# Scaled words of the weight decoder move from a PSUM bank of their own into the ring of the block maxima, the weight product gets both of its ring's banks, and the first stage is issued in another order

## The chip, the cores and the metric

The kernel runs on one core of a Trainium2 chip. The metric is device time in microseconds; 963.3 us is the median of three runs of the kernel before (961.33 to 964.49). The engines are named as the profile names them: PE is TensorE (PEld its weight loads), DVE is VectorE, ACT is ScalarE, POOL is GpSimd, and SP is the queue that issues the DMA transfers.

## The reference

Block-causal attention over 8 batches and 8 heads (576 rows, head width 64, blocks of 64), then a gated MLP without a nonlinearity, on the concatenated heads:

```python
scores = scale * np.matmul(q, k.transpose(0, 1, 3, 2))
scores = np.where(block_i >= block_j, scores, -1000000000.0)
scores = scores - np.max(scores, axis=-1, keepdims=True)
attn = np.exp(scores)
attn = attn / (np.sum(attn, axis=-1, keepdims=True) + 1e-09)
x = np.matmul(attn, v)          # (B, H, S, D), then (B*S, H*D)
a = x @ w1
b = x @ w2
h = a * b @ w3
out = h @ w_out
```

Since nothing nonlinear stands between `w3` and `w_out`, the kernel forms their product once.

## The kernel before

**Two stages.** Heads are handled in pairs, four pairs to a batch. In the first stage the program treats pairs 0 to 3 (batch 0) and prepares all weights; after it, pairs 4 to 31 run interleaved with the MLP of the batches before them, in which TensorE multiplies without a pause. The MLP's tiles are `ab` (line 503) and `o` (line 519).

**What the first stage does with weights.** The weights arrive as raw 64-bit words, in 40 units of 512 KB: 8 of `wout`, 16 of `w3t` (two for each of eight row blocks m), 8 of `w1`, 8 of `w2`. `load_w` (line 209) treats one unit in four steps: the transfer into a `wraw` buffer (a ring of five), ACT's scaled copy `y` of the high words (line 221), two byte fields that ACT and POOL write into `wbits` (lines 222 and 223; two buffers in turn), and DVE's shift-and-or that joins `y` and `wbits` into the float (line 224; a SCALAR_TENSOR_TENSOR in the profile). For `w1` and `w2` the result is split into a high half (POOL) and a low half (DVE), `w1h`, `w1l`, `w2h`, `w2l`. A `wraw` buffer can be refilled only when ACT and POOL have read it.

**What it does with the product.** `gen_prod` (line 474) forms, for each m, eight products over k of `w3` with `wo` in one PSUM bank, `acc`. ACT copies the bank to `wh`, DVE takes the rest `wl = acc - wh`. The next m that uses the same bank has to wait for `wl`.

**What it does with a pair.** The raw q, k, v arrive in one transfer. `shift_mask` (line 241) finds the block maxima: TensorE writes block scores to a PSUM bank of the ring `psq`, DVE reduces them into `m` (10 reductions a pair), TensorE transposes `m`, ACT negates it to `ms`. `prep_qk` (line 289) casts q and k and takes their low halves (`TENSOR_TENSOR qk<-raw,qk`), and shifts copies of them to the other 64 partitions by DMA (`qk<-qk`); for `ms` the same is done (`qk<-ms`). Then come the score tiles (`pss`, called S below), ACT's exponentials (`pe`), the products with v (`psx`), a transpose of the sums on DVE (`tr<-psx`), and the normalized `x32` with its halves `xh` and `xl`.

**PSUM.** Eight banks: two for `pss`, two for `psx`, two for `psq` (maxima), one, `psy`, for `y`, and one, `psm`, for `acc`. After the first stage `psm` and `psy` are used in turn by the MLP's tiles.

**What sets the order.** In the first stage every call of the engines is recorded, not issued. `ORDER`, a list of 768 call numbers written out by hand or by a search, then issues them (line 614); it sets the order on every engine and of the DMA transfers on SP, and, through `Later`, which buffer of a ring a call gets. Each engine takes its instructions in this order, and SP too: a transfer that must wait for an engine holds up all behind it. After the first stage the order comes from `PLAN` and, off TensorE, from the Tile scheduler.

```python
    def load_w(dst, src):
        t = new(tl["early"], [P, 1024], I32, tag="wraw", name="wraw", bufs=5)
        y = new(ps_m, [P, 512], F32, tag="psy", name="y")
```

Of the kernel before, what the change touches and what calls it, by code (L numbers as in the profile page):

```python
# [9 lines left out]
F32 = mybir.dt.float32  # L10
# [8 lines left out]
PSUM = bass.MemoryType.PSUM  # L19
OTHERS = {mybir.EngineType.Activation, mybir.EngineType.DVE, mybir.EngineType.Pool, mybir.EngineType.SP}  # L20

P = 128
# [39 lines left out]
)  # L62

ORDER = [int(k) for k in """
# [20 lines left out]
""".split()]  # L85

RING = {"raw": 2, "pss": 2, "psm": 1, "psy": 1, "psq": 2, "wraw": 5, "wy": 4, "w3": 2, "xh": 8, "xl": 8}

DELAY = 3

# [37 lines left out]
def block_causal_attention__then__gated_mlp_kernel(ctx, tc, qkv, consts, ident_in, w1, w2, w3t, wout, out_t):  # L128
# [5 lines left out]
    def new(pool, shape, dtype, tag, **k):  # L134
        if not isinstance(nc, Held):
            return pool.tile(shape, dtype, tag=tag, **k)
        return Later(lambda: slot(pool, shape, dtype, tag, **k))

    def slot(pool, shape, dtype, tag, name, **k):
        ring = rings[tag]  # L140
        n = RING.get(tag, 1)
        t = ring[-n] if len(ring) >= n else pool.tile(shape, dtype, tag=tag, name=tag, **k)
# [9 lines left out]
    ctx.enter_context(tc.manual_schedule(engines={mybir.EngineType.PE}))  # L152
    ps_s = ctx.enter_context(tc.tile_pool(name="ps_s", bufs=2, space=PSUM))
    ps_x = ctx.enter_context(tc.tile_pool(name="ps_x", bufs=1, space=PSUM))
    ps_m = ctx.enter_context(tc.tile_pool(name="ps_m", bufs=1, space=PSUM))
    ps_q = ctx.enter_context(tc.tile_pool(name="ps_q", bufs=2, space=PSUM))

    both = cpool.tile([P, 2 * P], F32, name="ident")
# [49 lines left out]

    def load_w(dst, src):
        t = new(tl["early"], [P, 1024], I32, tag="wraw", name="wraw", bufs=5)  # L210
        y = new(ps_m, [P, 512], F32, tag="psy", name="y")
        bits = tl["bits"][tl["unit"] % 2]
        tl["unit"] += 1
        nc.sync.dma_start(out=t, in_=src)
        high = t.rearrange("p (c two) -> p c two", two=2)[:, :, 1]
        byte = t.bitcast(U8).rearrange("p (c e) -> p c e", e=8)
        if dst is None:
            dst = new(tl["early"], [P, 512], F32, tag="wy", name="wy", bufs=4)
        low = bits.bitcast(U8).rearrange("p (c e) -> p c e", e=4)[:, :, 0]
        top = bits.bitcast(F8).rearrange("p (c e) -> p c e", e=4)[:, :, 3]  # L220
        nc.scalar.mul(out=y, in_=high.bitcast(F32), mul=2.0**-112)
        nc.scalar.activation(out=top, in_=byte[:, :, 7], func=AF.Copy, bias=127.5 * 2.0**-60, scale=-(2.0**-60), saturate=False)
        nc.gpsimd.tensor_scalar(out=low, in0=byte[:, :, 3], scalar1=1.0 / 32, scalar2=-31.0 / 64, op0=ALU.mult, op1=ALU.add)
        nc.vector.scalar_tensor_tensor(out=dst.bitcast(I32), in0=y.bitcast(I32), scalar=3, in1=bits, op0=ALU.logical_shift_left, op1=ALU.bitwise_or)
        return dst
# [258 lines left out]
            done[0] += 1  # L484
            yield

    turns = itertools.cycle(("psm", "psy"))

    def turn():
        return next(turns)  # L490

    def gen_moe(b):
        mp, gh, gl = tl["late"], tl["gh"], tl["gl"]
        for h in range(2):
            for f in range(NF):
                acc = []
                for a, b2 in ((w1h, w1l), (w2h, w2l)):
                    t = ps_m.tile([P, 512], F32, tag=turn(), name="ab")
                    fs = slice(f * P, (f + 1) * P)
                    for c in range(NC):  # L500
                        xh, xl = x_of[b, c, h]
                        for s, (l, r) in enumerate(((a, xh), (b2, xh), (a, xl))):
                            nc.tensor.matmul(t[:, 0:HALF], l[:, c, fs], r, start=(c == 0 and s == 0), stop=(c == NC - 1 and s == 2))  # L503
                        if c == 1 or (c == NC - 1 and len(acc) == 0):
                            yield
                    acc.append(t)
                a32 = mp.tile([P, HALF], F32, tag="a32", name="a32", bufs=2)
                nc.scalar.copy(a32, acc[0][:, 0:HALF])
                g32 = mp.tile([P, HALF], F32, tag="g32", name="g32", bufs=2)
                nc.vector.tensor_tensor(out=g32, in0=acc[1][:, 0:HALF], in1=a32, op=ALU.mult)  # L510
                nc.scalar.copy(gh[:, f, :], g32)  # L511
                nc.gpsimd.tensor_tensor(out=gl[:, f, :], in0=g32, in1=gh[:, f, :], op=ALU.subtract)  # L512
                yield
            for e in range(DM // P):
                t = ps_m.tile([P, 512], F32, tag=turn(), name="o")
                es = slice(e * P, (e + 1) * P)
                for f in range(NF):
                    for s, (l, r) in enumerate(((wh, gh), (wl, gh), (wh, gl))):
                        nc.tensor.matmul(t[:, 0:HALF], l[:, f, es], r[:, f, :], start=(f == 0 and s == 0), stop=(f == NF - 1 and s == 2))  # L519
                    if f % 2 and f < NF - 1:  # L520
                        yield
                o32 = mp.tile([P, HALF], F32, tag="o32", name="o32", bufs=2)
                nc.scalar.copy(o32, t[:, 0:HALF])
                nc.sync.dma_start(out=out_t[es, b * S + h * HALF : b * S + (h + 1) * HALF], in_=o32)
                yield
# [163 lines left out]
```

## Time and profile before

| | us |
|---|---|
| median of three runs | 963.3 |
| profiled execution, its own time | 965.79 |
| its span | 964.0 |
| first transfer is issued | 0.74 |
| transfers of the first stage | 29.44 MB until 132 us |
| PE busy in the span | 937.7 (97%) |
| DVE busy in the span | 692.4 (72%) |
| ACT busy | 550.2 (57%) |
| POOL busy | 612.4 (64%) |

The profiled execution took 1.8 us more outside its span, and 2.5 us more than the median. In the page's 40 slices of 24 us, TensorE's busy share is in tenths; a 9 in all slices but the first ones says that only the first five or so have idle time on that engine. In the waits view a row reads: engine and instruction that waited, what ended the wait, the total in microseconds, how often, the longest. In the chain view a row is a start, a duration and who held the chain. Line 124 is a helper's, so groups of the first stage are told apart by their tiles.

### The profile page before, as it was taken

To read this page: it belongs to the slowest core of one execution; us is meant where nothing else is said; L and a number is where in the kernel's file an instruction comes from. 1 tells how busy PE (TensorE), PEld (TensorE's weight loads), DVE (VectorE), ACT (ScalarE), POOL (GpSimd) and SP (SyncE) were. 2 spreads that over 40 slices of the span, in tenths; PEclk is the share of its full clock that TensorE was granted. 3 is DMA by queue.
4 is the path that set the end of the run, shared out by engine and by line. 5 is a ranking of instruction groups with operands and counts; after the bars stand their busy time and mean duration, and the time that the engine had idled before them with its cause. 6 is when DMAs were issued, how large, how long until landed. Compare 5 with 4: busy or idle time off the path is not lost.

```text
span 964.0 us, 18369 instructions
## 1 busy us (share of the span) xinstructions
PE 937.7 (97%) x6624; PEld 878.0 (91%) x6624; DVE 692.4 (72%) x1238; ACT 550.2 (57%) x1433; POOL 612.4 (64%) x614
## 2 busy tenths in 40 slices
PE   4889989999999999999999999999999999999998
PEld 2445569999999999999999999999999999999998
DVE  7768887778877777777887777777887877774100
ACT  5767655665666565565565655566556556553221
POOL 4667667676776767676777667676767767672211
PEclk9999999999999999999999999999999999999999
DMA  8668622222122222212122122312212222100000
GB/s 308 220 196 291 195 63 61 79 64 65 49 76 71 64 82 64 82 59 87 32 71 76 59 82 64 89 52 89 60 49 70 70 71 64 50 13 26 7 20 25
DMA packets 31261, 79.86 MB, mean 83 GB/s; under 512 B 5353, under 2 KB 13673, under 8 KB 31171
## 3 DMA queue, kind: packets, MB, share of 16 engines
q1 hardware_dynamic: 31171, 78.70, 26.4%
q8 instruction: 52, 0.85, 0.4%
q14 instruction: 38, 0.31, 0.1%
HBM read 50.76 MB, written 9.44 MB: 62 GB/s over the span
## 4 chain that ended last, share of the span: by engine, by line
PE 90%; DMA 5%; DVE 2%; ACT 2%; issue 1%; SPq 0%; POOL 0%; ACTq 0%; DVEq 0%; POOLq 0%
PE ab L503 42%; PE o L519 21%; PE s L334 9%; PE x L389 9%; PE mx L261 4%; PE psm L124 2%; DMA wraw<-in_w3t 2%; DMA wraw<-in_w 1%; PE psx L124 1%; DMA qk<-qk 1%; PE pss L124 1%; ACT psy L124 1%; ACT wbits L124 0%; PE tot L406 0%; SPq L124 0%
## 5 line engine op out<-in xcount | busy, mean ns | idle before, releaser
L355 POOL TENSOR_TENSOR rsum<-rsum,p 128x448 f32<-128x448 f32 x224 | 186.4, 832 | 87.5 <-ACT p L349 78.5
L352 DVE TENSOR_TENSOR pl<-p,ph 128x448 fp32r<-128x448 f32 x168 | 149.6, 904 | 60.8 <-ACT ph L350 59.9
L512 POOL TENSOR_TENSOR gl<-g,gh 128x288 fp32r<-128x288 f32 x128 | 114.4, 893 | 121.5 <-ACT gh L511 121.5
L503 PE MATMUL ab<-xh,w2h 128*128 128x288 f32 x512 | 153.7, 300 | 0.1
L519 PE MATMUL o<-gh,wh 128*128 128x288 f32 x512 | 153.5, 300 | 0.0
L503 PE MATMUL ab<-xh,w1h 128*128 128x288 f32 x512 | 151.2, 295 | 0.3 <-DVE wl L124 0.3
L503 PE MATMUL ab<-xl,w2h 128*128 128x288 f32 x512 | 151.1, 295 | 0.0
L503 PE MATMUL ab<-xh,w1l 128*128 128x288 f32 x512 | 150.9, 295 | 0.0
L503 PE MATMUL ab<-xl,w1h 128*128 128x288 f32 x512 | 150.9, 295 | 0.0
L503 PE MATMUL ab<-xh,w2l 128*128 128x288 f32 x512 | 150.9, 295 | 0.0
L519 PE MATMUL o<-gh,wl 128*128 128x288 f32 x512 | 150.9, 295 | 0.0
L519 PE MATMUL o<-gl,wh 128*128 128x288 f32 x512 | 150.8, 295 | 0.0
L304 POOL TENSOR_TENSOR qk<-raw,qk 64x1152 fp32r<-64x1152 f32 x54 | 144.2, 2671 | 2.0
L511 ACT CAST gh<-g 128x288 fp32r<-128x288 f32 x128 | 55.4, 433 | 143.2 <-DVE g L510 143.1
L350 ACT ACTIVATE ph<-s 128x288 fp32r<-128x288 f32 x336 | 131.3, 392 | 0.0
L334 PE MATMUL s<-qk 128*128 128x288 f32 (+4 forms) x672 | 129.6, 301 | 0.3 <-DMA qk<-ms 0.3
L349 ACT ACTIVATE p<-s 128x448 f32<-128x448 f32 x224 | 85.4, 381 | 51.1 <-PE s L334 50.3
L352 DVE TENSOR_TENSOR pl<-rsum,ph 128x288 fp32r<-128x288 f32 x112 | 76.3, 683 | 49.2 <-ACT ph L350 46.2
L389 PE MATMUL x<-ph,vs 128*128 128x128 f32 x336 | 110.3, 329 | 0.0
L265 DVE TENSOR_REDUCE m<-mx 128x1 f32<-128x512 f32 (+1 forms) x270 | 107.7, 448 | 1.7
L510 DVE TENSOR_TENSOR g<-ab,a 128x288 f32<-128x288 f32 x128 | 56.6, 442 | 69.3 <-PE ab L503 67.8
L334 PEld LDWEIGHTS s<-qk 128*128 128x128 f32 (+1 forms) x672 | 99.9, 179 | 1.9 <-DMA qk<-ms 0.9
(97 smaller groups left out, 2241.3 us busy)
## 6 DMA issues: line engine op xcount, KB each, us to landing
raw<-in_qkv SPq DMA_DIRECT2D x31, 896.0 KB
qk<-qk SPq DMA_DIRECT2D x124, 144.0 KB
out_t<-o SPq DMA_DIRECT2D x64, 144.0 KB
wraw<-in_w3t SPq DMA_DIRECT2D x16, 512.0 KB
wraw<-in_w SPq DMA_DIRECT2D x16, 512.0 KB
wraw<-in_wout SPq DMA_DIRECT2D x8, 512.0 KB
qk<-ms SPq DMA_DIRECT2D x62, 2.2 KB
raw<-in_qkv SPq DMA_DIRECT2D x2, 288.0 KB
```

What stands on the lines that cost most here:

```text
L265: nc.vector.reduce_max(m[:, col : col + 1], sc, axis=AX.X)
L304: (nc.gpsimd if "late" in tl or n * j else nc.vector).tensor_tensor(out=qk[j][o, 2:4], in0=rqk[o], in1=qk[j][o, 0:2], op=ALU.subtract)
L334: nc.tensor.matmul(t[ks, at : at + q1 - q0], qk[j][:, k, kr], qk[j][:, q, q0:q1], start=(s == 0), stop=(s == 1))
L349: nc.scalar.activation(p32, t[ks, at : at + w], AF.Exp, scale=SCALE)
L350: nc.scalar.activation(ph[ks, o : o + w], t[ks, at : at + w], AF.Exp, scale=SCALE)
L352: nc.vector.tensor_tensor(out=low, in0=p32, in1=ph[ks, o : o + w], op=ALU.subtract)
L355: nc.gpsimd.tensor_tensor(out=r, in0=r, in1=p32, op=ALU.add)
L389: nc.tensor.matmul(xps[:, to : to + w], v[:, c, :], pr[:, a : a + w], start=(u < 2 and s == 0), stop=(u in (0, len(PV) - 1) and s == len(p ...
L503: nc.tensor.matmul(t[:, 0:HALF], l[:, c, fs], r, start=(c == 0 and s == 0), stop=(c == NC - 1 and s == 2))
L510: nc.vector.tensor_tensor(out=g32, in0=acc[1][:, 0:HALF], in1=a32, op=ALU.mult)
L512: nc.gpsimd.tensor_tensor(out=gl[:, f, :], in0=g32, in1=gh[:, f, :], op=ALU.subtract)
L519: nc.tensor.matmul(t[:, 0:HALF], l[:, f, es], r[:, f, :], start=(f == 0 and s == 0), stop=(f == NF - 1 and s == 2))
```

## The change

Three things are changed. `y` is allocated from the ring `psq`, which the block maxima use, so the three uses (scores of the blocks, the transposed maxima, `y`) take turns in two banks; the tag `psy` is gone. The ring `psm` has two banks instead of one: the product uses them in turn in the first stage, and the MLP's tiles use the same two banks in turn afterwards, as before, without the helper that switched tags. And `ORDER` has the same 768 calls in another order.

```diff
-RING = {"raw": 2, "pss": 2, "psm": 1, "psy": 1, "psq": 2, "wraw": 5, "wy": 4, "w3": 2, "xh": 8, "xl": 8}
+RING = {"raw": 2, "pss": 2, "psm": 2, "psq": 2, "wraw": 5, "wy": 4, "w3": 2, "xh": 8, "xl": 8}
...
-    ps_m = ctx.enter_context(tc.tile_pool(name="ps_m", bufs=1, space=PSUM))
+    ps_m = ctx.enter_context(tc.tile_pool(name="ps_m", bufs=2, space=PSUM))
...
-        y = new(ps_m, [P, 512], F32, tag="psy", name="y")
+        y = new(ps_q, [P, 512], F32, tag="psq", name="y")
...
-    turns = itertools.cycle(("psm", "psy"))
-
-    def turn():
-        return next(turns)
-
...
-                    t = ps_m.tile([P, 512], F32, tag=turn(), name="ab")
+                    t = ps_m.tile([P, 512], F32, tag="psm", name="ab")
...
-                t = ps_m.tile([P, 512], F32, tag=turn(), name="o")
+                t = ps_m.tile([P, 512], F32, tag="psm", name="o")
...
 ORDER = [int(k) for k in """
-8 46 0 44 42 1 4 2 7 5 6 52 39 70 47 67 11 57 38 71 13 3 41 12 62 45 97 16 14 43 9 40 69 10 78 75 53 55 17 54 81 18 19 50 49 92 20 198 56 21 48 15 119
+8 46 0 4 1 42 3 6 7 5 2 44 52 39 70 47 11 57 38 71 13 62 41 67 40 92 12 22 23 9 75 43 84 24 30 10 31 45 25 33 18 19 54 55 32 21 14 20 49 50 15 26 27
```

What this does to the engines' order is shown at three places. **The DMA queue at the first half of the stage**, SP, before: transfers into `wraw` are weight units, `qk0<-qk0` is the shift of a pair's q and k that waits for DVE's cast of them, `raw` is the next pair.

```order
L124 DMA wraw_118<-in_w1 128x1024
L124 DMA wraw_124<-in_w3t 128x1024
L124 DMA raw_120<-in_qkv 128x1792
L124 DMA wraw_132<-in_w1 128x1024
L124 DMA wraw_135<-in_w3t 128x1024
L124 DMA wraw_114<-in_w3t 128x1024
L124 DMA qk0_86<-qk0_86 64x576
L124 DMA wraw_118<-in_w1 128x1024
L124 DMA qk0_86<-qk0_86 64x576
```

The same place now, from the transfer of pair 3 on to the shift of pair 2:

```order
L124 DMA raw_131<-in_qkv 128x1792
L124 DMA wraw_119<-in_w1 128x1024
L124 DMA wraw_123<-in_w1 128x1024
L124 DMA wraw_128<-in_w1 128x1024
L124 DMA wraw_134<-in_w1 128x1024
L124 DMA wraw_115<-in_w3t 128x1024
L124 DMA qk0_86<-qk0_86 64x576 x2
L124 DMA wraw_119<-in_w3t 128x1024
```

Before, 16 weight units were issued ahead of pair 2's shift, and the 17th stood behind it; now 21 are issued ahead of it.

**The end of the stage on TensorE**: `psm` is the product's bank, `w3` its left side, `psq<-ident` the transposed maxima of pair 4, `s4_0` the first scores of pair 4, `ab` the MLP's first tile. Before:

```order
L124 MATMUL psq_139<-kb_122,qd_90 128x448
L124 MATMUL psm_241<-wo_94,w3_385 128x512 x6
L124 MATMUL psq_137<-ident_81,m_153 9x128
L124 MATMUL psm_241<-wo_94,w3_385 128x512 x2
L334 MATMUL s4_0_932<-qk0_86 128x288 x2
L334 MATMUL s4_0_938<-qk0_86 128x288 x2
L503 MATMUL ab_944<-xh_380,w1h_82 128x288
```

Now:

```order
L124 MATMUL psm_352<-wo_94,w3_341 128x512
L124 MATMUL psm_221<-wo_94,w3_175 128x512
L124 MATMUL psm_352<-wo_94,w3_341 128x512
L124 MATMUL psq_137<-ident_81,m_146 9x128
L124 MATMUL psm_352<-wo_94,w3_341 128x512 x6
L334 MATMUL s4_0_932<-qk0_86 128x288 x2
L334 MATMUL s4_0_938<-qk0_86 128x288 x2
L498 MATMUL ab_944<-xh_361,w1h_82 128x288
```

Before, all eight products of m = 7 go to the one bank, behind `wl` of m = 6, and `ab` takes that bank again. Now m = 6 (`psm_221`) and m = 7 (`psm_352`) overlap, and `ab` takes the bank of m = 6.

**The same end on DVE**: `wl<-psm` empties a bank, `w3<-ps..` joins the last unit of `w3`, `x32` and `xl` finish pair 3, `qk0<-raw` is the low half of pair 4's q and k. Before:

```order
L124 SCALAR_TENSOR_TENSOR w3_385<-psy_150,wbits0_95 128x512
L124 CAST qk1_87<-raw_103 64x1152
L124 TENSOR_TENSOR wl_85<-psm_241,wh_84 128x512
L124 TENSOR_REDUCE m_153<-psq_137 128x1
L124 STREAM_TRANSPOSE tr_256<-psx_221 64x576
L124 SCALAR_TENSOR_TENSOR w3_385<-psy_150,wbits1_96 128x512
L124 TENSOR_REDUCE m_153<-psq_137 128x1
L124 TENSOR_TENSOR w2l_89<-wy_492,w2h_88 128x512
```

Now, from the last unit of `w3` on:

```order
L124 SCALAR_TENSOR_TENSOR w3_341<-psq_148,wbits1_96 128x512
L124 TENSOR_TENSOR w2l_89<-wy_481,w2h_88 128x512
L124 RECIPROCAL rr_266<-rr_266 128x18
L124 STREAM_TRANSPOSE tr_258<-rr_266 128x576
L124 TENSOR_TENSOR x32_272<-x32_272,tr_258 128x576
L124 TENSOR_TENSOR qk0_86<-raw_103,qk0_86 64x1152
L124 TENSOR_TENSOR wl_85<-psm_221,wh_84 128x512
L124 TENSOR_TENSOR xl_907<-x32_272,xh_900 128x288
L124 TENSOR_TENSOR wl_85<-psm_352,wh_84 128x512
```

The two halves of `w3` for m = 7 stood around the cast of pair 4 and `wl` of m = 6; now that `wl`, with pair 4's q and k, stands behind the last half.

38 rows, old and new, of the table ORDER are left out of this document.

## The prediction

> **What bounds the kernel now.** I read the slices first, then the busy times by stretch, cut where the first scores start (18.68) and where the MLP's first tile starts (132.25).
>
> ```profile
> span 964.0 us, 18369 instructions
> PE   4889989999999999999999999999999999999998
> 0.00:18.68 18.68, 5.12 (x16) 1.84 (x16) 12.66 (x21) 11.05 (x18) 9.84 (x17) 1.00 0.92 325
> 18.68:42.10 23.42, 22.16 (x88) 13.87 (x89) 19.39 (x36) 15.96 (x33) 12.37 (x12) 1.00 0.63 206
> 42.10:73.00 30.90, 25.88 (x83) 12.76 (x81) 21.29 (x36) 21.79 (x42) 19.80 (x25) 0.94 0.63 212
> 73.00:105.37 32.37, 32.37 (x118) 18.44 (x119) 28.83 (x49) 24.96 (x50) 24.41 (x28) 1.00 0.79 276
> 105.37:120.80 15.43, 14.81 (x52) 7.83 (x50) 11.10 (x18) 8.89 (x17) 8.06 (x10) 1.00 0.58 179
> 120.80:132.25 11.45, 9.29 (x26) 4.28 (x26) 9.24 (x17) 6.00 (x14) 5.98 (x7) 1.00 0.11 26
> 132.25:964.00 831.75, 828.05 (x6245) 819.02 (x6245) 589.91 (x1067) 461.60 (x1263) 531.92 (x518) 1.00 0.21 61
> ```
>
> The columns are the stretch, its length, busy time of PE, PEld, DVE, ACT, POOL, granted clock, DMA share, GB/s. Behind 132.25 TensorE is busy 828.05 of 831.75 us, so that part moves as a block: **the change is worth what it moves the start of `ab`**. In the first stage no engine is full. DVE is the fullest over it: 12.66 + 19.39 + 21.29 + 28.83 + 11.10 + 9.24 = 102.5 of 132.25 us. TensorE, from 18.68 on, is busy 104.5 of 113.6 us, a busy time that holds stretched matmuls. So this stage is bound by waits between engines that each take a fixed order. The chain says which end last:
>
> ```profile
> 8.83 8.96 DMA qk<-qk
> 18.68 0.85 PE pss L124 x2
> 105.37 8.06 DMA wraw<-in_w
> 122.86 0.70 DVE wl L124
> 123.61 5.42 PE psm L124 x12
> 132.25 1.86 PE ab L503 x12
> ```
>
> The start is held by a small transfer (8.96 us) that lands behind those issued before it. Later a weight unit that took 8.06 us to land holds it, and at the end TensorE begins m = 7 of the product at 123.61, the moment `wl` has emptied the only bank.
>
> **The start: 0.** Eleven transfers up to that `qk<-qk` are the same set in the new order, with the constants a little earlier; its landing is set by their bytes, and DVE needs only about 12 of its 17.8 us until then. I take no change up to 18.68.
>
> **The end of the stage: -2.3 us.** DVE's last rows, with their waits in brackets:
>
> ```profile
> 124.59 0.69 DVE L124 SCALAR_TENSOR_TENSOR w<-psy,wbits 128x512 int32<-128x512 int32 x1
> 125.66 0.68 DVE L124 TENSOR_TENSOR w2l<-wy,w2h 128x512 fp32r<-128x512 f32 x1
> 126.58 0.27 DVE L124 RECIPROCAL rr<-rr 128x18 f32<-128x18 f32 x1
> 127.37 0.77 DVE L124 STREAM_TRANSPOSE tr<-rr 128x576 f32<-128x576 f32 x1
> 128.24 0.76 DVE L124 TENSOR_TENSOR x<-x,tr 128x576 f32<-128x576 f32 x1
> 129.59 0.65 DVE L124 TENSOR_TENSOR xl<-x,xh 128x288 fp32r<-128x288 f32 x1 [0.59 <-POOL xh L124]
> 131.51 0.69 DVE L124 TENSOR_TENSOR wl<-psm,wh 128x512 fp32r<-128x512 f32 x1 [1.27 <-ACT wh L124]
> L124 DVE TENSOR_TENSOR qk<-raw,qk 64x1152 fp32r<-64x1152 f32 x6 | 8.7, 1457 | 0.1
> ```
>
> From the join of the last `w3` unit (124.59) to `ab` (132.25) it takes 7.66 us now, most of it one bank's chain: `wl` of m = 6, eight products, `wh`, `wl` of m = 7. With two banks, m = 7's first four products run before that join and four behind it: 4 x 2 x 0.45 (5.42 / 12 for one of the two passes of a product) = 3.6 us, ending 0.69 + 3.6 = 4.3 us behind the join's start. Meanwhile DVE does the join, `w2l`, reciprocal, transpose, `x`, and pair 4's low half, which now stands here: 0.69 + 0.68 + 0.27 + 0.77 + 0.76 + 1.46 = 4.6 us. Pair 4's four first scores then take some 0.7 us, and `wl` of m = 6 0.69 us beside them; `ab` no longer waits for `wl` of m = 7. So 5.4 us in place of 7.66. The other half, `xl` and the last `wl`, stands behind: if `ab` found it in its way, it would cost 0.65 + 0.69 = 1.3 us.
>
> **The join itself: from 124.59 to 120.1, -4.5 us.** DVE must do its work ahead of the join, and the rest is idle time. Now: 102.5 less 5.7 behind 124.59 is 96.8 of work, so 27.8 idle. Then: 102.5 less 6.4 is 96.1. The waits that make the idle time, until 132:
>
> ```profile
> DVE wl L124 <- ACT wh L124: 4.1, 3, 2.4
> DVE qk L124 <- PE pss L124: 3.1, 4, 1.1
> DVE wy L124 <- ACT wbits L124: 2.9, 1, 2.9
> DVE w L124 <- ACT psy L124: 2.3, 2, 1.7
> DVE wy L124 <- POOL wbits L124: 2.1, 3, 0.9
> DVE m L124 <- PE psq L124: 1.8, 2, 1.5
> DVE w L124 <- POOL wbits L124: 1.1, 2, 0.7
> PE psm L124 <- DVE wl L124: 3.6, 4, 2.2
> SPq L124 <- DVE qk L124: 26.7, 7, 13.9
> ```
>
> - Start, until 18.68: 18.68 - 12.66 = 6.0. Stays.
> - Weight units (`wy`, `w` behind `wbits`, `psy`): 2.9 + 2.3 + 2.1 + 1.1 = 8.4. They are late because their transfers are issued late: SP stood 26.7 us behind DVE's casts. In the new order four units of `w1` and one of `w3t` go ahead of pair 2's shift. Following the rows by hand from 18.68, each at the end of what it waits for, with the durations above and 7 us for a unit to land, I get these moments:
>
> ```profile
> 52.12 0.56 SPq L124 DMA_DIRECT2D wraw<-in_w  x1
> 57.34 0.81 SPq L124 DMA_DIRECT2D wraw<-in_w  x2
> 107.27 1.56 SPq L124 DMA_DIRECT2D wraw<-in_w3t  x2
> ```
>
>   the 17th unit at 41 in place of 52.12, the 20th at 49 in place of 57.34, the 40th at 103 in place of 107.27. I take 2.7 of the 8.4 as left (-5.7). If nothing came earlier, this term is 0.
> - `wl` behind `wh`: 4.1, less the 1.27 that lies behind the join, 2.8. In the new order `wl` of m = 2 to 5 stand several rows behind their `wh`; 0 left (-2.8).
> - DVE behind TensorE: 3.1 + 1.8 = 4.9. This grows. Two rows of the new order stand across: the transpose of pair 0's second head stands ahead of the first `w3` unit of m = 1, while TensorE first does three products that wait for `wo` (by hand 3.5 us of DVE idle, near 35 to 38), and a reduction for pair 3 waits behind scores whose shift has just been issued (3.4 us, near 73 to 77). With five shorter ones I get 9.6 (+4.7).
> - All else: 27.8 - 6.0 - 8.4 - 2.8 - 4.9 = 5.7, taken as it is.
>
> That is 6.0 + 2.7 + 0 + 9.6 + 5.7 = 24.0 of idle and 96.1 of work: 120.1. (By hand alone the join came at 117.5; the hand count has no gap between an engine's end and the next one's start, and I leave 2.6 us for that and for landings beyond 7 us.)
>
> **The shared ring.** `y` and the maxima now take turns in two banks. The trace of before shows no such sharing. Between two units it helps: ACT's copy into the one bank `psy` waited for DVE's join of the unit before. Between a unit and a maximum it hurts: the block scores, on TensorE, wait for a join on DVE that waits for a landing, and all matmuls queue behind.
>
> ```profile
> ACT psy L124 <- DMA wraw<-in_w: 4.0, 2, 3.4
> ACT wbits L124 <- DMA wraw<-in_w3t: 4.1, 2, 2.2
> ACT wbits L124 <- DMA wraw<-in_w: 3.1, 3, 1.9
> ACT psy L124 <- DMA wraw<-in_w3t: 1.0, 1, 1.0
> ```
>
> ACT waited 12.2 us for landings. The price of sharing lies between 0 (every unit has landed when its turn comes) and +12.2 (each of these waits reaches TensorE). I take it inside the 9.6 above, since with units issued 4 to 11 us earlier most have landed; 12.2 is kept for the range. The product's second bank is worth between 0 and the 3.6 us that `psm` waited for `wl`; 2.2 at most of it is already in the tail.
>
> A transfer's time is thus the number that matters most: 8.06 us above for one unit. The Trainium skill (DMA: Bandwidth & Descriptors, Anatomy of one DMA — SWDGE (gpsimd) path) fits 2.0 us plus bytes over 436 GB/s on the GpSimd path, an estimate of 3.2 us for 512 KB. By that hardly a unit would be late, and the 5.7 us would not be there to win: the outcome that the second rival below prices from rows. Here SP issues, and the row says 8.06, with the DMA share at 0.58 to 0.79; the row decides.
>
> TensorE's clock is 0.94 in 42.10:73.00, 1.00 elsewhere: 0.06 x 30.9 = 1.9 us at most, behind its waits there. The Trainium skill (TensorE: Matmul & The Clock Gate, Part 1: The HAM clock gate) says that an idle window of about 3.4 us halves the clock. By that rule the new order, whose longest TensorE wait by hand is 1.9 us, would win these 1.9 us back, as the first rival below has it, and one gap more would lose as much again; the sum counts neither.
>
> **Sum.** -2.3 - 4.5 = -6.8: `ab` at 125.5. The profiled execution took 965.79, so 959.0 on its own scale; it lies 2.5 above the median of 963.3, so the median goes to **956.5 us**.
>
> **The rivals.**
> - *Larger gain:* TensorE becomes the bound and only its busy time is left. It idled 113.6 - 104.5 = 9.1 us; with these and the clock's 1.9 gone, -11.0: 952.3. For it: DVE's work alone would allow 102.5 plus 6.0. Against: the two places where DVE stands behind TensorE in the new order.
> - *Landings eat it (the order does not do what it says):* units are issued earlier but land no earlier, since the transfers queue (share 0.79 in one stretch already), and only the tail is won: 963.3 - 2.3 = 961.0. For it: the DMA must move the same 29 MB in less time.
> - *Slower:* the shared ring. Landings beyond 10 us at one unit after another keep its bank, the maxima of the next pair wait on TensorE, and with them the product and the scores. All 12.2 us reach TensorE; the tail's 2.3 and the 5.7 stay won: 963.3 + 12.2 - 8.0 = 967.5. It decides from landings 3 us longer than the 7 counted. Against: only one landing in the chain is over 8 us, the start's apart.
>
> **How the numbers follow.** Forecast 0.57 (its own range 953.5 to 960), larger gain 0.13, landings 0.18, slower 0.12. A measurement of this kernel tells about 0.3%, 2.9 us, from no change: faster 0.57 + 0.13 = 0.70, same 0.18, slower 0.12. The range takes in the third case, most of the second and none of the fourth: 950 to 965.
>
> **What would show it.** Right: the start of `pss` at 18.7 still; SP's row for pair 2's shift with 21 units ahead of it; `ab` at 123 to 128; no `ab` or `psm` wait for `wl` over 1 us; the `psq` rows on PE waiting for a join under 3 us in total. Wrong: `ab` near 130, with DVE waiting for `wbits` as long as before (landings); or rows of `psq` on TensorE waiting for `w`, `wo` or `wy` for over 8 us (the ring); or a start later than 18.7, which I count at nothing.

## The result and the profile after

| | before | after |
|---|---|---|
| median of six runs (range) | 963.92 us (961.33 to 966.02) | 957.88 us (955.76 to 960.38) |
| profiled execution, its span | 965.79, 964.0 | 956.89, 955.1 |
| first scores (`pss` behind the small transfer) | 18.68 | 19.18 |
| last `w3` unit's join, start | 124.59 | 119.04 |
| first tile of the MLP, `ab` | 132.25 | 124.29 |

The ratio is 0.9936, its 95% interval 0.9921 to 0.9952: 6.0 us less between the medians, 8.9 between the two profiled executions. Of these 8.9, 8.0 lie ahead of `ab` (132.25 to 124.29) and 0.9 behind it (831.75 to 830.81). Here and below `ab` starts where the chain has it; TensorE's own row of it, which overlaps the scores ahead, starts at 132.25 and 124.13. First the head of the page of the changed kernel and its slices, then its busy times by stretch, with the columns of before:

```profile
span 955.1 us, 18369 instructions
PE   3999999999999999999999999999999999999998
```

```profile
0.00:18.37 18.37, 4.26 (x13) 1.48 (x13) 12.17 (x19) 11.83 (x19) 9.30 (x17) 1.00 0.91 316
18.37:42.10 23.73, 21.29 (x77) 12.68 (x78) 16.77 (x29) 16.79 (x34) 13.19 (x14) 1.00 0.67 227
42.10:124.29 82.19, 81.89 (x292) 44.26 (x291) 73.86 (x123) 60.93 (x117) 58.38 (x66) 1.00 0.70 222
124.29:955.10 830.81, 827.50 (x6246) 818.68 (x6244) 589.77 (x1069) 462.14 (x1265) 532.86 (x519) 1.00 0.21 61
```

The third row is the news: from 42.10 to `ab`, 82.19 us, TensorE is busy for 81.89; before, it was busy for 82.35 of the 90.15 us from 42.10 to `ab`. That an engine is full is not new in itself: the prediction read "no engine is full" over the whole stage, but its row 73.00:105.37 had TensorE busy for 32.37 of 32.37. VectorE is busy for 73.86 of the same 82.19. The chain of waits at the end of the stage:

```profile
8.41 9.87 DMA qk<-qk
...
118.15 5.33 PE psm L124 x12
...
123.50 0.80 PE s L334 x4
124.29 1.66 PE ab L498 x12
```

TensorE's twelve passes of the product end at 118.15 + 5.33 = 123.48. VectorE's rows at that place:

```profile
119.04 0.69 DVE L124 SCALAR_TENSOR_TENSOR w<-psq,wbits 128x512 int32<-128x512 int32 x1 [0.66 <-POOL wbits L124]
...
122.10 1.34 DVE L124 TENSOR_TENSOR qk<-raw,qk 64x1152 fp32r<-64x1152 f32 x1
123.37 0.68 DVE L124 TENSOR_TENSOR wl<-psm,wh 128x512 fp32r<-128x512 f32 x1
123.97 0.45 DVE L124 TENSOR_TENSOR xl<-x,xh 128x288 fp32r<-128x288 f32 x1
124.34 0.68 DVE L124 TENSOR_TENSOR wl<-psm,wh 128x512 fp32r<-128x512 f32 x1
```

Pair 4's low half, which the first scores of pair 4 read, ends at 122.10 + 1.34 = 123.44, 0.04 us from TensorE's end; `xl` and the last `wl` stand behind and hold nothing. The waits of VectorE that the prediction split up, in the first 124.3 us (total, times, longest), and in a second fence those of TensorE from 18 us on (ahead of that, its `psq` waited another 1.7 us for `w`):

```profile
DVE m L124 <- PE psq L124: 5.1, 8, 1.9
DVE tr L124 <- PE psx L124: 2.5, 2, 2.3
DVE w L124 <- POOL wbits L124: 1.3, 2, 0.7
DVE wy L124 <- POOL wbits L124: 0.7, 1, 0.7
DVE qk L124 <- PE pss L124: 0.4, 1, 0.4
```

```profile
PE pss L124 <- DVE qk L124: 5.4, 1, 5.4
PE psq L124 <- DVE w L124: 1.6, 1, 1.6
PE psq L124 <- DVE wy L124: 0.2, 1, 0.2
```

There is no row of `wl` behind `wh`, and none of `ab` or `psm` behind `wl`. SP's issues of the units that moved:

```profile
44.46 5.44 SPq L124 DMA_DIRECT2D wraw<-in_w  x4
52.60 0.33 SPq L124 DMA_DIRECT2D wraw<-in_w3t  x1
52.98 1.17 SPq L124 DMA_DIRECT2D qk<-qk  x2
...
103.86 0.33 SPq L124 DMA_DIRECT2D wraw<-in_w3t  x1
```

The four are the units 17 to 20, the next is the 21st, then comes pair 2's shift; the row at 103.86 is the 40th unit.

### The profile page after: what moved, and what is told of

Its sections match the earlier page's. It is cut to its first block, busy times and chain, and to the rows that moved or that the text cites. A ratio compares the mean times of both kernels' runs of the same rounds, so it can differ in the third digit from the quotient of the medians.

```text
span 955.1 us, 18369 instructions
## 1 busy us (share of the span) xinstructions
PE 934.9 (98%) x6624; PEld 877.1 (92%) x6624; DVE 692.6 (73%) x1238; ACT 551.7 (58%) x1433; POOL 613.7 (64%) x614
## 4 chain that ended last, share of the span: by engine, by line
PE 96%; DMA 2%; DVE 1%; POOL 0%; issue 0%; SPq 0%; ACT 0%; DVEq 0%; POOLq 0%; ACTq 0%
PE ab L498 43%; PE o L514 22%; PE s L334 9%; PE x L389 9%; PE psm L124 5%; PE mx L261 4%; PE psx L124 2%; PE pss L124 1%; DMA qk<-qk 1%; PE psq L124 1%; DMA raw<-in_qkv 1%; PE tot L406 0%; DMA wraw<-in_w 0%; PE mt L269 0%; DVE tr L124 0%
```

## The experiments

The start turned out to move from run to run, so I compare **the stretch**: from VectorE's first half of pair 0's constants (`qk<-ms,qk 9x576`, the row that waits for the small transfer) to `ab`. For the two kernels:

```profile
17.88:132.25 114.37, 104.60 (x364) 57.17 (x363) 90.62 (x152) 77.59 (x153) 70.66 (x81) 0.99 0.62 207
```

```profile
18.37:124.29 105.92, 103.18 (x367) 56.94 (x368) 90.64 (x151) 77.72 (x150) 71.58 (x79) 1.00 0.69 223
```

Before 114.37, after 105.92: 8.45 us less. All runs in one table; "tail" is from the last `w3` unit's join to `ab`, and times are medians where there are several runs. Row, `ab`, stretch and tail are each read from one profile, and how far a stretch scatters from run to run was not measured; thirteen runs of the kernel before lay between 959.51 and 967.13 us. So a difference of 1 to 3 us between two stretches is a reading and not a proof.

| kernel | row | `ab` | stretch | tail | time (runs) |
|---|---|---|---|---|---|
| before | 17.88 | 132.25 | 114.37 | 7.66 | 963.92 (6) |
| after | 18.37 | 124.29 | 105.92 | 5.25 | 957.88 (6) |
| one bank | 18.25 | 135.00 | 116.75 | 6.96 | 969.31 (10) |
| one bank's order, two banks | 17.17 | 129.51 | 112.34 | 5.18 | 963.75 (10) |
| shift first | 17.38 | 126.03 | 108.65 | 5.26 | 959.14 (10) |
| after, less TensorE | 16.60 | 122.70 | 106.10 | 5.26 | 955.37 (1) |
| after, less VectorE | 17.29 | 123.31 | 106.02 | 5.31 | 957.05 (1) |
| after, less of both | 17.04 | 121.59 | 104.55 | 5.25 | 955.17 (1) |
| after, fewer transfers | 17.62 | 121.67 | 104.05 | 6.06 | 954.54 (1) |
| after, fewer transfers, less TensorE | 17.42 | 121.06 | 103.64 | 5.26 | 953.63 (1) |
| before, less TensorE | 17.30 | 127.50 | 110.20 | 8.34 | 960.87 (1) |
| before, less VectorE | 16.51 | 127.35 | 110.84 | 7.79 | 960.79 (1) |
| small transfer ahead of four | 16.77 | 124.88 | 108.11 | 5.27 | 956.78 (7) |
| small transfer ahead of two | 16.24 | 122.67 | 106.43 | 5.26 | 956.17 (5) |

**The product's second bank.** The changed kernel with one bank for the product; the products of m stand behind `wl` of m - 1, `wh` right behind the last product, `wl` six places later:

```diff
-RING = {"raw": 2, "pss": 2, "psm": 2, "psq": 2, "wraw": 5, "wy": 4, "w3": 2, "xh": 8, "xl": 8}
+RING = {"raw": 2, "pss": 2, "psm": 1, "psq": 2, "wraw": 5, "wy": 4, "w3": 2, "xh": 8, "xl": 8}
```

> The changed kernel with one bank for the product instead of two: the products of m stand behind wl of m-1, each wh right behind its last product, each wl six places later; all else in the changed order. Theory 'the bank carries the tail' (the sum on record): the 7.66 us from the last w3 unit's join to the first tile of the MLP come back in place of 5.25, and TensorE again waits for wl (3.6 us before): that first tile starts 2 to 6 us later than 124.29, time 2 to 6 us longer. Rival 'the order carries it all' (the weight units' earlier issue): within 1 us of the changed kernel in both.

969.31 us (ratio to the runs of before beside it 1.0062, 1.0039 to 1.0085): 11 us slower than the changed kernel, and slower than before. `ab` came 10.7 us later, beyond what either theory allowed. Its waits on VectorE, and on TensorE:

```profile
DVE m L124 <- PE psq L124: 12.7, 10, 2.2
DVE wl L124 <- ACT wh L124: 8.6, 6, 2.6
```

```profile
PE psm L124 <- DVE wl L124: 6.3, 4, 2.0
```

TensorE stands 6.3 us for `wl`, VectorE 8.6 for `wh`, and the maxima, queued on TensorE behind the waiting products, now keep VectorE 12.7 in place of 5.1. But order and bank were changed at once, so the next kernel has that order word for word, and two banks:

```diff
-RING = {"raw": 2, "pss": 2, "psm": 1, "psq": 2, "wraw": 5, "wy": 4, "w3": 2, "xh": 8, "xl": 8}
+RING = {"raw": 2, "pss": 2, "psm": 2, "psq": 2, "wraw": 5, "wy": 4, "w3": 2, "xh": 8, "xl": 8}
```

> The order of the one-bank run word for word, but with two banks for the product: nothing but the bank differs between the two. Theory 'the bank itself costs it' (TensorE waits for each wl before the next m's products): the 10.7 us by which the MLP's first tile came later with one bank go, the tile at 124 to 127. Rival 'the order written for one bank costs it': the tile stays at 131 to 135, and the bank by itself is worth less than 4 us.

Between the two expectations: 963.75 us, stretch 112.34. With the same order **the bank alone is worth 116.75 - 112.34 = 4.4 us** of the stretch (5.6 between the medians): 1.8 of it in the tail, 2.6 ahead of the join, where the product no longer waits (TensorE has no `psm` row left). **The order that only two banks allow is worth another 6.4** (112.34 to 105.92; 5.9 between the medians). How the two share is uncertain by some 1.7 us: the profile in the middle holds 3.41 us at half the granted clock (40.52 to 43.93), and the other two hold no such spell behind 26 us, so that 4.4 is rather too low and 6.4 too high. How good the best order for one bank would be is not shown; the one of before, written for one bank, reached 114.37. The ring change was not run with the order of before, in which `y` and the maxima would overwrite each other; so what `y` gains from two shared banks in place of one of its own is not known by itself.

**The units ahead of pair 2's shift.** Four of the five units that the change put ahead of it go back behind it: the 17th and the 19th to the 21st (312, 335, 342 and 370 in the list), not the 17th to the 20th as the expectation says. The 18th (305) stays ahead. Parts of the list's lines:

```diff
-... 203 220 312 279 ...
+... 203 220 279 ...
...
-... 259 335 268 ...
+... 259 268 ...
...
-... 333 342 272 ...
+... 333 272 ...
...
-... 392 370 231 303 332 300 295 331 334 ...
+... 392 231 303 332 300 295 331 312 335 342 370 334 ...
```

> The changed kernel with the transfers of four weight units (the 17th to the 20th, issued at 44.46 in the changed kernel) moved behind pair 2's shift (52.98), where they stood before the change; nothing else moves. Theory 'earlier issue wins the weight units' waits' (-5.7 us in the sum on record): VectorE and ScalarE wait for these units again, the MLP's first tile starts 2 to 5 us later. Rival 'TensorE is the bound from 42 us on and has other work': its busy share stays above 98% from 42 us on and the tile starts within 1 us.

SP's rows, then what VectorE, ScalarE and TensorE waited for:

```profile
44.50 0.38 SPq L124 DMA_DIRECT2D wraw<-in_w  x1
51.15 1.17 SPq L124 DMA_DIRECT2D qk<-qk  x2
52.43 1.48 SPq L124 DMA_DIRECT2D wraw<-in_w  x3
```

```profile
DVE m L124 <- PE psq L124: 8.1, 9, 1.9
ACT psq L124 <- DMA wraw<-in_w: 1.9, 1, 1.9
PE psx L124 <- ACT x L124: 1.2, 1, 1.2
PE pss L124 <- DMA qk<-qk: 2.1, 2, 1.0
```

The stretch grew by 2.7 us to 108.65, with 959.14 us against 957.88 (ratios to before 0.9945, 0.9926 to 0.9965, and 0.9936: not told apart by the times). VectorE's extra wait is not where the prediction put it: `wy` and `w` wait for 2.0 us, as in the changed kernel, and the maxima for 8.1 in place of 5.1. The other rows, none of which the changed kernel has, show the way there. ScalarE's copy `y` waits 1.9 us for the landing of a late unit (until 56.57), its copy `x` of a product with v stands behind, TensorE waits 1.2 us for that (until 57.82), and the maxima behind on TensorE come late. The shared ring is not in it: TensorE's `psq` waits for joins as long as before the edit (1.9 us for 1.8). Of the 2.7 us, 1.0 was already lost by 41.9 us, ahead of the place of the edit, behind the landing of another shift (one of the two waits in the last row).

**Which engine bounds the stage.** In the changed kernel one product in eight is left out for m = 2 to 7 (the output lacks these terms):

```diff
+SKIP = [395, 463, 563, 621, 721, 753]
...
         for k in ORDER:
+            if k in SKIP:
+                continue
```

> The changed kernel without one of the eight products of each m from 2 to 7 (six products, 12 matmul passes of 0.45 us, 5.3 us of TensorE's work; the output is therefore not the reference's). Theory 'TensorE is the bound': the MLP's first tile starts 4 to 5.3 us earlier than 124.29. Rival 'TensorE and VectorE's chain end together, bound jointly': at most 1.5 us earlier, and TensorE idles 3 us and more between 42 and the tile.

`ab` came 1.6 us earlier, but the small transfer had landed 1.8 earlier. The stretch:

```profile
16.60:122.70 106.10, 99.44 (x355) 54.26 (x356) 90.70 (x151) 77.01 (x150) 72.87 (x81) 1.00 0.71 227
```

It is 106.10, as long as with all products: TensorE's idle time in it rose from 2.74 to 6.66 us, by new waits for the landings of shifts (1.3 and 0.8 us) and for joins (0.8) among others. So an engine that is busy for 81.89 of 82.19 us is not, by that alone, what a saving shortens. Then VectorE:

```diff
-                nc.vector.reduce_max(m[:, col : col + 1], sc, axis=AX.X)
+                nc.vector.reduce_max(m[:, col : col + 1], sc[:, 0:16] if isinstance(nc, Held) else sc, axis=AX.X)
```

> The changed kernel with each block maximum of the early stage taken over the first 16 columns of a score tile only (some 13.6 us less of VectorE's work between 18.4 and the MLP's first tile, by the reductions' rows; the row maxima and so the output are not the reference's). Measured from the first scores (19.18 in the changed kernel) to the MLP's first tile (124.29), 105.1 us. Theory 'VectorE bounds the stage now' (it is what is left after a run without 5.3 us of TensorE's work moved that stretch by nothing): 6 us and more shorter. Rival 'TensorE's full busy rows are the bound': at most 2 us shorter. Third, 'neither alone, the landings and the order': at most 2 us shorter, and VectorE idle for as much longer as its work is less.

```profile
17.29:123.31 106.02, 102.40 (x368) 56.86 (x369) 78.33 (x151) 76.89 (x149) 75.00 (x79) 0.97 0.71 227
```

VectorE had 90.64 - 78.33 = 12.3 us less to do in the stretch, which stayed at 106.02: the third expectation. Both edits at once:

> The changed kernel without the 5.3 us of TensorE's products and without the 13.6 us of VectorE's reductions at once (one of eight products of each m from 2 to 7 left out, block maxima over 16 columns). From the first half of pair 0's constants (VectorE's row at 18.37 in the changed kernel) to the MLP's first tile (124.29) it took 105.9 us, 106.1 without the one and 106.0 without the other. Theory 'two chains side by side, each covers the other': 3.5 to 6 us shorter. Rival 'a third thing holds both, the landings of the weight units or the issue on SyncE': at most 1.5 us shorter.

```profile
17.04:121.59 104.55, 98.74 (x355) 54.46 (x356) 78.34 (x151) 76.48 (x150) 73.79 (x79) 0.97 0.73 230
```

1.4 us shorter, with TensorE 4.4 and VectorE 12.3 us less busy than in the changed kernel: the rival's range, by which a third thing holds both. The transfers of the last 28 weight units are left out next, with the decoder's work all there (it works on what its buffer held):

```diff
+SKIP = [218, 225, 258, 263, 312, 305, 335, 342, 370, 415, 375, 438, 420, 498,
+    491, 445, 526, 521, 570, 575, 584, 591, 622, 704, 629, 679, 672, 709]
```

> The changed kernel without the transfers of the last 28 of the 40 weight units (from 36.16 us on; the decoder then works on what its buffer held, so that the output is not the reference's); all of the decoder's work stays. Stretch from VectorE's row at 18.37 to the MLP's first tile, 105.9 us. Theory 'landings and SyncE's issue hold the stage': 4 us and more shorter. Rival 'the units are early enough now' (the sum on record left 2.7 us of waits for them, the trace shows 2.7 to 3.2): 1.5 to 3.5 us shorter. Third, 'TensorE's and VectorE's chains hold it': at most 1.5 us shorter.

```profile
17.62:121.67 104.05, 101.22 (x368) 56.70 (x369) 89.28 (x151) 77.34 (x150) 72.26 (x79) 1.00 0.29 88
```

1.9 us shorter, the second expectation: by this profile the landings, and SP's waits to issue them, cost no more by themselves. The same without the six products as well:

> The changed kernel without the last 28 units' transfers and without the 5.3 us of TensorE's products together (the decoder works on what its buffer held, one of eight products of each m from 2 to 7 is left out). The stretch was 105.9 with both, 104.1 without the transfers, 106.1 without the products, 104.6 without the products and 13.6 us of VectorE's work. Theory 'three chains within 2 us of each other: TensorE, VectorE, landings': 102 to 104, VectorE's is the one left. Rival 'with the landings gone TensorE alone is the bound': 98.5 to 101.

```profile
17.42:121.06 103.64, 98.33 (x355) 54.19 (x356) 89.85 (x151) 76.94 (x150) 71.60 (x80) 1.00 0.30 90
```

2.3 us shorter, within the first expectation. No cut gave more than that. Several chains of nearly the same length, each of which covers the others, would explain it; which one was left at the end is not shown, since all three cuts at once were not tried.

The kernel before, with the same two cuts:

> The kernel before, without one of the eight products of each m from 2 to 7 (5.3 us of TensorE's work; the output is not the reference's). From the first scores (18.68) to the MLP's first tile (132.25), 113.6 us. Theory 'waits between engines in fixed orders bound it': at most 2 us shorter. Rival, 'one bank ties the product's own time into the chain' (each m's products must lie between two wl): 3 to 5.3 us shorter.

```profile
17.30:127.50 110.20, 100.49 (x353) 54.80 (x352) 90.25 (x152) 77.75 (x153) 72.98 (x81) 0.98 0.65 216
```

> The kernel before, with the block maxima taken over the first 16 columns only (some 13.6 us less of VectorE's work; the output is not the reference's). From the first scores (18.68) to the MLP's first tile (132.25), 113.6 us. Theory 'VectorE's own time plus a fixed idle time sets the join' (the sum on record): 9 to 13 us shorter. Rival 'the waits for landings and for the bank set it': at most 4 us shorter.

```profile
16.51:127.35 110.84, 104.96 (x366) 57.56 (x364) 78.72 (x152) 77.83 (x153) 73.49 (x80) 0.98 0.66 218
```

Here the products are worth 114.37 - 110.20 = 4.2 us, most of their 5.3, which fits that with one bank their own time stands between two `wl`. VectorE's 90.62 - 78.72 = 11.9 us are worth 3.5. These are single runs, and their times (960.87 and 960.79) lie within those of the kernel before. Both rivals' ranges held; "VectorE's own time plus a fixed idle time" fell.

**The small transfer.** Four, and then two, of the large transfers ahead of the small `qk<-qk` (58.5 KB) go behind it. Parts of the list's lines in the diff with two (raw of pair 1, a `wout` unit):

```diff
-... 13 62 41 67 40 92 12 ...
+... 13 62 41 40 12 ...
...
-... 30 10 31 ...
+... 30 10 67 92 31 ...
```

> The changed kernel with four large transfers (raw of pair 1 and three wout units, 2 MB and more) issued behind the small transfer qk<-qk instead of ahead of it. Theory 'the small transfer waits for the bytes ahead of it, and TensorE is the bound from 42 us on, so that a start gained is kept': qk<-qk lands 2 to 6 us earlier than 18.28, the first scores start at 16.5 to 17.5 instead of 19.18, and the MLP's first tile starts 1 to 2.5 us earlier, time 1 to 2.5 us less. Rival 'the landing moves but the stage gets it back': the first scores earlier as above, the tile within 0.5 us of 124.29 or later, since raw of pair 1 and the wout units land later and TensorE idles for them between 20 and 42.

> The changed kernel with two large transfers only (raw of pair 1 and the third wout unit) issued behind the small qk<-qk instead of ahead of it. In the runs so far the row at which VectorE takes that landing lay between 16.5 and 18.4 us, and the stretch from it to the MLP's first tile stayed the same (105.9 to 106.1 where the work was the changed kernel's or less), but became 108.1 when four transfers were moved behind. Theory 'the start is kept one for one, as long as no unit lands late for it': the row at 15.8 to 17, the stretch 106 to 107, the tile at 122 to 123.5, time 1 to 2 us under the changed kernel's 957.9. Rival 'the stretch takes it back': the stretch 107.5 or more, time 957 to 959.

VectorE's row in the changed kernel, then with four, then with two:

```profile
18.37 0.75 DVE L124 TENSOR_TENSOR qk<-ms,qk 9x576 fp32r<-9x576 f32 x1 [1.84 <-DMA qk<-qk]
```

```profile
16.77 0.75 DVE L124 TENSOR_TENSOR qk<-ms,qk 9x576 fp32r<-9x576 f32 x1 [0.56 <-ACT ms L124]
```

```profile
16.24 1.10 DVE L124 TENSOR_TENSOR qk<-ms,qk 9x576 fp32r<-9x576 f32 x1
```

In both the wait for the landing is gone. With four moved, the `wout` units land late, and GpSimd waits for them:

```profile
POOL wbits L124 <- DMA wraw<-in_wout: 4.3, 2, 4.1
```

The stretch takes it back (108.11, `ab` at 124.88: the rival), and the time, 956.78 us, is not told from the changed kernel's. With two moved the stretch is 106.43, and the start is kept. **956.17 us in five runs (955.55 to 956.86), ratio to the runs of before beside it 0.9904, 0.9888 to 0.9921**: what the first theory said, 1.7 us below the changed kernel's median, though the two were not run side by side and their intervals (0.9921 to 0.9952 there) touch. A part of the lower ratio is the kernel before, whose median beside these five runs was 965.23.

## Why the prediction was right, and where it was not

The median was forecast at 956.5 us and came at 957.88; on the profile's own scale 959.0 was forecast and 956.89 measured, since `ab` moved by 8.0 and not by 6.8. The end of the stage was right in its mechanism. That the rest came out so near is in part luck, as the three steps below show.

**The start, taken as 0:** +0.5 us between the two profiles (first scores 18.68 to 19.18), one of the signs of being wrong. The landing scatters by more: in the twelve profiles with the transfer at its old place the row lay between 16.51 and 18.37. Where the work was the changed kernel's or less of one engine's, the stretch behind it was the same within 0.2 us (105.92, 106.10, 106.02), and 106.43 with the two transfers moved, so a late landing seems to go nearly one for one into `ab`. So the start is no reason why the two profiled executions differ by more (-8.9) than the medians (-6.0): the changed kernel's profile has the latest row of the twelve.

**The end of the stage, -2.3:** 7.66 to 5.25, -2.4. The two sides were counted at 4.3 us on TensorE and 4.6 on VectorE from the join on; both took 4.4.

**The join, 120.1:** 119.04. Forecast and measured idle time of VectorE until then, from the window rows and waits above:

| | before | forecast | after |
|---|---|---|---|
| start | 6.0 | 6.0 | 18.37 - 12.17 = 6.2 |
| weight units (`wy`, `w`) | 8.4 | 2.7 | 1.3 + 0.7 = 2.0 |
| `wl` behind `wh` | 2.8 | 0 | 0 |
| behind TensorE (`m`, `tr`, `qk`) | 4.9 | 9.6 | 5.1 + 2.5 + 0.4 = 8.0 |
| all else | 5.7 | 5.7 | 5.2 |
| idle time | 27.8 | 24.0 | 21.4 |

(0.2 of the 5.1 lies ahead of 18.37 and so is counted in the start as well.)

VectorE's work until the join is 97.62 us in the windows' row, and so its idle time 119.04 - 97.62 = 21.4:

```profile
0.00:119.04 119.04, 102.21 (x366) 56.22 (x367) 97.62 (x163) 87.03 (x165) 78.38 (x92) 1.00 0.75 247
```

The term that was mis-sized is VectorE behind TensorE, 8.0 for 9.6; of its two rows the transpose came out at 2.3 us (3.5 by hand), and the reduction near 73 to 77 (3.4 by hand) shows no wait; the longest wait of a maximum, 1.9 us, ended at 25.23. The work ahead of the join was 1.5 us more than the 96.1 counted, which took over half of the difference back.

**The issue of the units:** the 17th was put at 41 and came at 44.46, the 20th, forecast for 49, lies in the row that ends at 49.90, the 40th came at 103.86 (103). 21 units ahead of the shift, as said. `psq` on TensorE waited 3.5 us for joins in all, a little over the 3 that were named as a sign; 1.7 of it lies ahead of 18 us, where the landing of the small transfer holds the start anyway.

**Where the reasoning failed though the sum held.** Three steps:

- *"VectorE must do its work ahead of the join, and the rest is idle time"*, with all else taken as it is, treats the idle time as fixed. The runs with less of VectorE's work show that it is not: 11.9 us less work gave 3.5 before and nothing after; the rest became waits. The sum came out because the change happened to leave VectorE's work nearly alone (90.62 and 90.64 us in the stretch).
- *The second bank, "between 0 and the 3.6 us", 2.2 of it in the tail:* 4.4 us in one order, 2.6 of them ahead of the join, and the orders that it allows 6.4 more. The prediction gave most of the gain ahead of the join, 5.7 us, to the units' earlier issue. Moving four units back cost 2.7 of the stretch at most, by way of ScalarE's and TensorE's order and not at `wy` and `w`. Those waits did fall from 8.4 to 2.0, as forecast, but they stayed at 2.0 with the four units back: why they fell stays open, and so does what the earlier issue of the other units is worth.
- *"Larger gain: TensorE becomes the bound"* was given 0.13, at -11.0. Its rows came true (81.89 of 82.19 us), its price did not: 8.0 before `ab`. Nor is TensorE alone the bound: 5.3 us less of its work left the stretch at 106.10. That TensorE, VectorE and the landings hold the stage together is what the cuts suggest; none of them gave more than 2.3 us.

**The clock.** It was 0.94 in 42.10:73.00 before and 1.00 in 42.10:124.29 after, as the rival with the 1.9 us had it. The 0.94 is one spell: from 46.54 to 49.95 the granted clock was 0.50, and its four passes of the product, which waited for `wl`, took 3.60 us (four took 1.88 at 42.01):

```profile
46.67 3.60 PE L124 MATMUL psm<-wo,w 128*128 128x512 f32 x4 [2.23 <-DVE wl L124]
```

The runs give an estimate of its share. Of 47 runs of the kernel before that stand beside the experiments, ten have a mean granted clock of 0.999 or 1.000 and a median of 961.4 us, 22 have 0.997 or 0.998 and 964.3, and 15 have less and 966.2. Of the changed kernel's six runs five have 0.999 or 1.000, with a median of 957.5. At the full clock the two are thus 3.9 us apart, and about 2 of the 6.0 us lie in spells that the changed kernel has less often. That the wait for the one bank brings the spells on is not shown.

**The other rivals.** No `ab` near 130, no VectorE waits for landings as before: the second rival is out, and the shared ring's 12.2 us did not come.

## What to carry to other kernels

In a stage bound by waits between engines, busy time does not price an edit. Here 11.9 us less of VectorE's work gave 3.5 before and 12.3 less gave nothing after, while the change, which left that work alone, gave 8.45 of the stretch. A wait that an edit removes is no safe price either: the rest of the stage decides how much of it turns up as another wait. When such a stage has become even, a full row in the windows says only that an engine may be one of the limits; leave its work out for one run before tuning it. And look at the first landing: a small transfer issued behind large ones decided the start, and two places in the queue brought the row that waits for it from 18.37 to 16.24.

## What the runs showed of the hardware

**A small transfer waits for the bytes ahead of it.** The 58.5 KB took 9.87 us from its issue at 8.41 in the changed kernel. With two large transfers (1.44 MB) moved behind it, the last semaphore mark of its landing stands at 13.50 in the trace, 5.4 us behind its issue; with four (2.49 MB) at 11.36, 2.8 us behind. That is 4.45 us less for 1.44 MB and 7.06 less for 2.49 MB, some 320 to 350 GB/s (an estimate from these numbers), close to the 316 GB/s of the window row 0.00:18.37. The Trainium skill (DMA: Bandwidth & Descriptors, Two DMAs through the same engine are not ordered) says that descriptors of one queue on one engine start in order; these rows agree.

**The clock column says 1.00 also where the trace has no record.** TensorE stands still ahead of the first scores, for 5.4 us in the changed kernel and 5.2 in the run with shorter reductions. Busy times and clock in 19 to 23 us, in the one and in the other:

```profile
19.00:23.00 4.00, 3.77 (x14) 2.86 (x15) 3.30 (x7) 1.90 (x5) 2.10 (x2) 1.00 1.01 412
```

```profile
19.00:23.00 4.00, 3.95 (x14) 2.58 (x14) 1.57 (x5) 2.89 (x7) 1.95 (x2) 0.50 1.00 407
```

The column has 1.00 in one and 0.50 in the other, but TensorE gets through 14 matmuls in both. Two passes of the product in the changed kernel, at two places:

```profile
22.85 1.91 PE L124 MATMUL psm<-wo,w 128*128 128x512 f32 x2
29.06 1.02 PE L124 MATMUL psm<-wo,w 128*128 128x512 f32 x2
```

At 22.85 they took nearly twice as long, so the clock was about half there in the changed kernel too. The trace's clock records begin at 25.73 in it, at 22.64 in the kernel before and at 10.78 in the run with shorter reductions; ahead of them the column is no measurement, and neither is the prediction's 1.00 there. So none of the differences between stretches above is put down to the 0.50 in the early part of three of the profiles.

**Where there are records, half the clock lasts 3.41 us or three times that.** It was 46.54 to 49.95 in the kernel before, 40.52 to 43.93 with the one bank's order, and 14.19 to 24.43 with shorter reductions. The Trainium skill (TensorE: Matmul & The Clock Gate, Part 1: The HAM clock gate) has a window of 3.413 us that runs free of the program; these lengths agree with it. The prediction went by an idle window, but ahead of the spell in the kernel before TensorE was busy for 1.31 of 3.41 us (43.13 to 46.54).
